# Reciprocals of the softmax sums: VectorE's reciprocal out of PSUM, or ScalarE's exp of minus ln with a Newton step

## The chip, the core and the metric

The kernel runs on one core of one Trainium2 chip. Its engines work through queues of their own and wait for each other by semaphores: TensorE (PE in the profile; its weight loads are PEld), VectorE (DVE), ScalarE (ACT), GpSimd (POOL) and SyncE (SP), which here only issues transfers (DMA). The metric is the time of one execution on the device in microseconds.

## The reference

Two blocks follow each other. The first is attention over 4 batches, 8 heads, 768 positions and 64 dimensions per head, in which a query sees only the keys whose hash (6 bits from a random projection) is equal to its own:

```python
q_bits = (np.einsum('bhsd,dk->bhsk', q, proj) > 0).astype(np.int64)
k_bits = (np.einsum('bhsd,dk->bhsk', k, proj) > 0).astype(np.int64)
...
scores = np.where(q_bucket[:, :, :, None] == k_bucket[:, :, None, :], scale * (q @ k.T), -1e9)
attn = np.exp(scores - np.max(scores, axis=-1, keepdims=True))
attn = attn / (np.sum(attn, axis=-1, keepdims=True) + 1e-09)
x = attn @ v
```

The second block is an MLP mixer on the result, put together as 4 x 768 x 512: `u = x + (relu(x.T @ w_tok1) @ w_tok2).T` over the positions, then `u + relu(u @ w_ch1) @ w_ch2` over the channels. The result is float32; the weights come as 64-bit numbers and are converted on the core.

## The kernel before, in words

The heads are worked on two at a time: 16 pairs of heads, numbered n. Fourteen of them go through the main loop of `attention` (L998), one turn each; the other two ("sorted") are computed by another method whose pieces are put between the turns. After the loop come the token block and the channel block of the mixer, which take the rest of the time (the attention ends at about 300 us).

A pair's 768 queries are worked on in two halves of 384 (`Half`). For each half there are six blocks of 128 keys, and a block holds both heads: 128 keys x (2 x 384) queries, with the keys on the partitions. One turn of the loop issues, in this order, to each engine's queue:

- `scores` (L484 to L518): TensorE computes the twelve blocks of scores into PSUM (L501), ScalarE turns each into exponentials in SBUF (`exponential`, L412). A score block takes a slot of the ring of four PSUM slots (`bank_pair`, L269, tag `sc`, `bufs=4`). The second block is cut in two pieces, so there are thirteen such slots a turn.
- `add` and `add_last` (L444 to L457): VectorE adds up the exponentials over the six blocks of each half, so that 128 partial sums per query are left (`esd`).
- `sums` (L528): for the pair before, TensorE multiplies the partial sums with a matrix of ones (L534). The result `ps` (named `hash` in the profile, after its slot of the same ring) is 128 partitions x 384: four groups of 32 equal rows, in the order head 0 half 0, head 0 half 1, head 1 half 0, head 1 half 1. The other bank of this slot takes the hash bits of the next pair (`Hash`, L342), which VectorE reads (`spread`, L364 and L365) and DMAs spread.
- `sums` ends on ScalarE: `near = exp(-ln(ps))` (L538, L539).
- `newton` (L542): VectorE makes a Newton step on `near` (L547, L549), and ScalarE copies rows of 32 partitions (L555) so that every one of the 128 rows has the reciprocals of both halves. `rec` is 128 x 2 x 384. In the turns 6 and 10, which hold pieces of the sorted pairs, `newton` is called earlier (L1029), ahead of `add_last` and of transposes on VectorE.
- `weigh` (L459) for half 0 and later for half 1: TensorE multiplies the exponentials with the values into the accumulator `acc` (L468), which takes the next slot of the same ring. ScalarE takes the numerators out of it (`vsum` L477, `num` L478).
- Between them VectorE converts a piece of a weight matrix from 64-bit numbers to float32 (`weights.join`, L187 to L196, and `weights.end`, L206), and it forms the quotients (`divide`, L559) for the pair before. In every other turn it transposes results for a bounce through memory (`bounce`, L233).

A PSUM slot is used anew once its readers are through. So the slot of the sums comes free when `newton` has read it, and that of the accumulator when the numerators are out. The order of the queues is the order in which this Python code issues the instructions; nothing reorders it.

The signs are arranged around the Newton step: it gives minus the reciprocal, since `(t - 2) * near` with `t = ps * near` is negative, and so the numerators are taken with `scale=-1.0` (L479), and a constant in the column that is summed along with the values is `-EPS` (L979).

Of the kernel before, what the change touches and what calls it, by code (L numbers as in the profile page):

```python
# [36 lines left out]
F32 = mybir.dt.float32  # L37
# [4 lines left out]
ALU = mybir.AluOpType  # L42
ACT = mybir.ActivationFunctionType
# [5 lines left out]
def kernel(  # L49
# [16 lines left out]
    nc = tc.nc  # L66
    P = 128
    B, NP, _, _, S = qk.shape
    D = 64
# [8 lines left out]
    HALF = S // 2  # L78
# [10 lines left out]
    EPS = 2.0**-70  # L89
# [168 lines left out]
    def attention(pool, psum, W1, W2, x0):  # L258
        first_bits = x0.rearrange("p r c -> p (r c)")[:, :S].bitcast(BF16).rearrange("p (w s) -> p w s", w=2)
        bitrows = [pool.tile([P, S + HALF], BF16, name=f"bits{n}", tag=f"bits{n}", bufs=1) for n in range(2)]  # L260
        exps = pool.tile([P, 2 * NR, 2, HALF + 1], F32, name="exps", tag="exps", bufs=1)
# [7 lines left out]
        def bank_pair(name):  # L269
            return psum.tile([P, 2, 512], F32, name=name, tag="sc", bufs=4)  # L270

        def load_qk(n):
            if n >= NREG:
                return
            b, hp = pairs[n]
            t = pool.tile([P, 2 * (S + HALF)], F32, name="qk", tag="qk", bufs=3)
            if n:
                nc.sync.dma_start(out=t, in_=qk_rows[b, hp])
            else:
                t = t[:, : 2 * S].rearrange("p (w s) -> p w s", w=2)  # L280
                for i in (1, 0):
                    nc.sync.dma_start(out=t[:, i, :HALF], in_=qk[b, hp, :, i, :HALF])
                nc.sync.dma_start(out=t[:, :, HALF:], in_=qk[b, hp, :, :, HALF:])
            loaded[n] = [t, None, None]
# [14 lines left out]
        def apart(made, group):  # L299

            tc.declare_no_dep(made.ins, group=group, reason="another bank of the same tile")
# [100 lines left out]
        class Half:  # L402
# [56 lines left out]
            def weigh(self, to):  # L459

                _, vn, vsum = loaded[self.n]
                columns = HALF if self.half else HALF + 1
                acc = to[:, self.half, :columns]
                for c in range(NR):
                    e = exps[:, NR * self.half + c, :, :columns]
                    for i in range(2):
                        for d in range(0, D, 32):
                            made = nc.tensor.matmul(  # L468
                                acc[D * i + d : D * i + d + 32], vn[:, i, c, d : d + 32], e[:, i],
                                start=(c == 0), stop=(c == NR - 1),  # L470
                            )
                            if self.half:
                                apart(made, f"num{self.n}")
                if self.half == 0:
                    nums[self.n] = pool.tile([P, 2, HALF], F32, name="num", tag="num", bufs=2)
                    vsum = loaded[self.n][2] = pool.tile([P, 1], F32, name="vsum", tag="vsum", bufs=2)
                    tc.add_to_no_dep_group(f"num{self.n}", nc.scalar.copy(vsum, acc[:, HALF:]).ins)  # L477
                made = nc.scalar.activation(  # L478
                    nums[self.n][:, self.half], acc[:, :HALF], ACT.Identity, scale=-1.0, bias=vsum,  # L479
                )  # L480
                if self.half == 0:
                    tc.add_to_no_dep_group(f"num{self.n}", made.ins)
# [37 lines left out]
        nums = {}  # L520

        class Quotients:
# [5 lines left out]
            def sums(self, ps):  # L528

                ps = ps[:, :HALF]  # L530
                for i in range(2):
                    for h in range(2):
                        at = 32 * (2 * i + h)
                        nc.tensor.matmul(  # L534
                            ps[at : at + 32], ones, self.halves[h].d[:, i], start=True, stop=True,
                        )
                near = pool.tile([P, HALF], F32, name="near", tag="near", bufs=1)
                tc.add_to_no_dep_group(f"sums{self.n}", nc.scalar.activation(near, ps, ACT.Ln).ins)  # L538
                nc.scalar.activation(near, near, ACT.Exp, scale=-1.0)  # L539
                self.ps, self.near = ps, near  # L540

            def newton(self):  # L542

                ps, near = self.ps, self.near
                rec = self.rec = pool.tile([P, 2, HALF], F32, name="rec", tag="rec", bufs=1)
                t = rec[:, 1]
                nc.vector.tensor_tensor(t, ps, near, op=ALU.mult)  # L547
                for h in range(2):
                    nc.vector.scalar_tensor_tensor(  # L549
                        rec[:, h], t, 2.0, near, op0=ALU.subtract, op1=ALU.mult,  # L550
                    )
                for i in range(2):
                    for h in range(2):
                        at, other = D * i + 32 * h, D * i + 32 * (1 - h)
                        nc.scalar.copy(rec[other : other + 32, h], rec[at : at + 32, h])  # L555

            def divide(self):
                b, hp = pairs[self.n]
# [33 lines left out]
        sorting, made = pool.tile([P, sum(widths.values())], F32, name="sorting", tag="sorting", bufs=1), {}  # L592
# [383 lines left out]

        nc.scalar.preload_act_table_set("natural_log_exp_and_others")
        nc.vector.memset(first_bits[:, 0], 0.0)
        nc.gpsimd.memset(exps[:, :, :, HALF:], -EPS)  # L979
        load_qk(1)  # L980
        constants = prepare_bits()

# [1 line left out]
        for _ in range(6):  # L984
# [6 lines left out]
            bufs=2,  # L991
# [6 lines left out]
        for n in range(NREG):  # L998
# [26 lines left out]
            acc = bank_pair("acc")  # L1025
# [1186 lines left out]
    def attention_and_tokens(W1, W2, x0):  # L2212
        inside(attention, W1, W2, x0)
        pool = late.enter_context(tc.tile_pool(name="late", bufs=1, side="right", reuse_waits="tile"))
        SW1 = big["SW1"] = pool.tile([P, 3, NCB // 2, DCH // 2], F32, name="SW1")
        TA = big["TA"] = pool.tile([P, 2, NCB // 2, TT], F32, name="TA")
        n = NHT * DM

        def second_tile(i):
            return pool.tile([P, (n, n * 3 // 4)[i]], F32, name=f"second{i}", tag=f"second{i}", bufs=1)  # L2220

        WC2 = second["WC2"] = second_tile(0).rearrange("p (k c) -> p k c", k=NHT)
        second["SW2"] = second_tile(1).rearrange("p (i k c) -> p i k c", i=3, k=NHT // 2)
        second["tile"] = second_tile

        def weights(pool):
            return Conversion(pool, [(w_ch2, WC2, 3, (0, NHT))], bufs=3)

        def jobs(conversion):
            early, late = weight_sums(  # L2230
                WC1, SW1, slice(0, NCB // 2), slice(NCB // 2, NCB), slice(0, DCH // 2), slice(DCH // 2, DCH),
            )
            return [
                lambda: (early(), late()),
                *[conversion.one] * (NHT * DM // NW),
            ]

        SW2 = second["SW2"].rearrange("p i k c -> p i (k c)")
        places = [SW2[:, i] for i in range(3)]
        inside(tokens, W1, W2, x0, weights, jobs, [TA[:, 0], None, TA[:, 1], None], places)  # L2240
# [100 lines left out]
```

## Time and profile before

| What | Value |
|---|---|
| median of 2 runs | 774.15 us (772.04 to 776.27) |
| the profiled execution | 774.78 us |
| its span on the core | 773.0 us |
| granted TensorE clock | 1.0 |
| busy: PE, PEld | 758.4 us, 507.7 us |
| busy: DVE, ACT, POOL | 673.6 us, 443.4 us, 187.7 us |
| exponentials L412 on ScalarE | 126.0 us in 181 instructions |
| copies L555 on ScalarE | 28.5 us in 56 instructions |

The span is the time from the first to the last instruction that the profile shows; the time of the execution is 1.8 us longer. A group's row in the profile names the line, the engine, the operation, the tile written and the tiles read, the shapes and the count; then the busy time in us and the mean of one in ns, and after the bar the time for which the engine stood idle just before these instructions, with what ended it. A row of the order in time has the start in us from the start of the span, the length in us, and the same names; rows that follow each other and are alike are merged, with their count, so that the length covers them all and the small gaps between. A TensorE row's end is modelled, and neighbouring matmuls overlap.

### The profile page before, as it was taken

To read this page: it belongs to the slowest core of one execution; us is meant where nothing else is said; L and a number is where in the kernel's file an instruction comes from. 1 tells how busy PE (TensorE), PEld (TensorE's weight loads), DVE (VectorE), ACT (ScalarE), POOL (GpSimd) and SP (SyncE) were. 2 spreads that over 40 slices of the span, in tenths; PEclk is the share of its full clock that TensorE was granted. 3 is DMA by queue.
4 is the path that set the end of the run, shared out by engine and by line. 5 is a ranking of instruction groups with operands and counts; after the bars stand their busy time and mean duration, and the time that the engine had idled before them with its cause. 6 is when DMAs were issued, how large, how long until landed. Compare 5 with 4: busy or idle time off the path is not lost.

```text
span 773.0 us, 14558 instructions
## 1 busy us (share of the span) xinstructions
PE 758.4 (98%) x5549; PEld 507.7 (66%) x5549; DVE 673.6 (87%) x965; ACT 443.4 (57%) x826; POOL 187.7 (24%) x248
## 2 busy tenths in 40 slices
PE   8999999999999999999999999999999999999997
PEld 4555556565556554455444468888877888886886
DVE  5798999899998998999687798998899799889884
ACT  5576777777777773333222326566766666675331
POOL 2306760547752530011211101210000221000001
PEclk9999999999999999999999999999999999999999
DMA  7455488654765479795696996899576695850565
GB/s 254 173 194 152 153 254 264 177 186 143 164 249 118 143 187 249 265 228 96 113 333 213 345 391 233 254 246 267 171 222 208 235 242 147 241 157 7 203 155 132
DMA packets 129802, 157.80 MB, mean 204 GB/s; under 512 B 56000, under 2 KB 99520, under 8 KB 127808
## 3 DMA queue, kind: packets, MB, share of 16 engines
q1 hardware_dynamic: 115664, 127.32, 51.9%
q0 software_dynamic: 12528, 28.86, 15.9%
q8 instruction: 45, 0.74, 0.4%
q10 hardware_dynamic: 1536, 0.65, 0.3%
q14 instruction: 29, 0.24, 0.1%
HBM read 107.71 MB, written 40.67 MB: 192 GB/s over the span
## 4 chain that ended last, share of the span: by engine, by line
PE 49%; issue 20%; DVE 16%; DMA 6%; SPq 4%; POOL 2%; ACT 2%; DVEq 0%; POOLq 0%; ACTq 0%
PE b L1323 27%; PE sc L501 9%; PE acc L468 7%; DVE esd L457 2%; DMA seen<-in_qk 1%; PE sc L423 1%; DVE size L196 1%; POOL seen L2140 1%; DVE unit L195 1%; SPq L238 1%; PE sacc L873 1%; DMA qk<-in_qk_rows 1%; SPq L919 1%; SPq L806 1%; DMA XT<-second 1%
## 5 line engine op out<-in xcount | busy, mean ns | idle before, releaser
L1323 PE MATMUL b<-R,second 128*128 128x256 f32 (+1 forms) x522 | 132.0, 409 | 0.8 <-ACT c L1329 0.8
L412 ACT ACTIVATE exps<-sc 128x768 f32<-128x768 f32 (+1 forms) x181 | 126.0, 765 | 5.9 <-PE sc L501 3.8
L501 PE MATMUL sc<-qk 32*128 32x384 f32 (+1 forms) x1352 | 119.5, 457 | 0.0
L1323 PEld LDWEIGHTS b<-R,second 128*128 128x128 f32 x522 | 99.0, 190 | 29.7 <-issue 16.5
L468 PE MATMUL acc<-exps,vn 128*32 128x385 f32 (+1 forms) x1344 | 111.7, 486 | 0.0
L501 PEld LDWEIGHTS sc<-qk 32*128 32x128 f32 x1352 | 92.7, 185 | 15.0 <-issue 3.2
L1329 ACT COPY c<-b 128x256 f32<-128x256 f32 (+1 forms) x96 | 40.2, 426 | 79.3 <-PE b L1323 66.1
L468 PEld LDWEIGHTS acc<-exps,vn 128*32 128x32 f32 x1344 | 43.7, 109 | 61.7 <-issue 60.0
L457 DVE TENSOR_TENSOR esd<-esd,exps 128x768 f32<-128x768 f32 x70 | 67.0, 958 | 6.8 <-DVE esd L457 1.0
L789 POOL DMA_INDIRECT table<-XT,sorting x48 | 60.8, 1266 | 23.7 <-issue 11.0
L377 POOL DMA_DIRECT2D bits<-XT x78 | 38.8, 504 | 108.7 <-DVE XT L365 56.5
L1323 PE MATMUL b<-XT,WC 128*128 128x256 f32 (+1 forms) x208 | 61.0, 428 | 0.0
L501 PE MATMUL sc<-bits 32*128 32x384 bf16 (+1 forms) x338 | 49.1, 311 | 0.7 <-ACT num L478 0.6
L1323 PEld LDWEIGHTS b<-XT,WC 128*128 128x128 f32 x208 | 39.5, 190 | 15.4 <-issue 10.3
L1323 PE MATMUL b<-XT,SW 128*128 128x256 f32 (+1 forms) x164 | 47.0, 410 | 0.0
L453 DVE TENSOR_TENSOR esd<-esd,exps 128x768 f32<-128x768 f32 x42 | 40.3, 960 | 4.4
L1196 PE MATMUL t<-x,W 128*128 128x512 f32 x96 | 42.1, 594 | 0.3 <-DMA x<-bounced 0.3
L2140 POOL DMA_DIRECT2D seen<-in_qk x21 | 13.0, 618 | 108.0 <-ACT seen L2130 71.8
L555 ACT COPY rec<-rec 32x384 f32<-32x384 f32 x56 | 28.5, 510 | 16.4 <-DVE rec L549 13.3
L1323 PEld LDWEIGHTS b<-XT,SW 128*128 128x128 f32 x164 | 31.1, 190 | 9.4 <-issue 4.1
L2033 POOL DMA_DIRECT2D out<-second x7 | 8.7, 1243 | 113.2 <-ACT TB L1329 73.9
L177 ACT ACTIVATE size<-raw 128x768 f32<-128x768 f32 x20 | 18.7, 935 | 26.8 <-DMA bits<-XT 16.2
(330 smaller groups left out, 1458.3 us busy)
## 6 DMA issues: line engine op xcount, KB each, us to landing
second<-left SPq DMA_DIRECT2D x20, 768.0 KB
qk<-in_qk_rows SPq DMA_DIRECT2D x13, 1152.0 KB
raw<-in_moe_w_ch SPq DMA_DIRECT2D x16, 768.0 KB
second<-left SPq DMA_DIRECT2D x18, 576.0 KB
seen<-in_qk POOLq DMA_DIRECT2D x21, 384.0 KB, 5.3
WC<-hidden_left SPq DMA_DIRECT2D x18, 448.0 KB
x<-bounced SPq DMA_DIRECT2D x4, 1536.0 KB
XT<-second POOLq DMA_DIRECT2D x8, 768.0 KB, 6.5
```

The costliest lines, as they stand in the source:

```text
L377: queue.dma_start(out=to[at : at + 2 * BITS, half[j]], in_=g[of : of + 2 * BITS])
L412: return nc.scalar.activation(e[:, :, columns], sc, ACT.Exp, scale=SCALE)
L453: nc.vector.tensor_tensor(self.d, self.d, e, op=ALU.add)
L457: nc.vector.tensor_tensor(self.d, self.d, e, op=ALU.add)
L468: made = nc.tensor.matmul(acc[D * i + d : D * i + d + 32], vn[:, i, c, d : d + 32], e[:, i], start=(c == 0), stop=(c == NR - 1),)
L501: nc.tensor.matmul(made[j, piece][:, i], k[at : at + 32, ks], q[at : at + 32], start=part < 0, stop=part == 1,)
L555: nc.scalar.copy(rec[other : other + 32, h], rec[at : at + 32, h])
L789: nc.gpsimd.indirect_dma_start(out=tables[2 * w + i], out_offset=bass.IndirectOffsetOnAxis(ap=self.at[:, x : x + 1], axis=0), in_=row, in_ ...
L1196: nc.tensor.matmul(ps, W1[:, r, P * j : P * j + P], x[:, r], start=(r == 0), stop=(r == NR - 1),)
L1323: nc.tensor.matmul(ps, left(k), right(k), start=start and k == ks[0], stop=stop and k == ks[-1], skip_group_check=True,)
L1329: nc.scalar.copy(c, ps)
L2140: nc.gpsimd.dma_start(out=t, in_=qk[pairs[n][0], pairs[n][1], :, i])
```

## The change

The logarithm, the exponential and the Newton step give way to VectorE's reciprocal operation, which reads the sums in PSUM once, for 128 partitions x 384 elements, and writes into one half of `rec`. The row copies on ScalarE are ordered anew, since now one instruction has written the reciprocals of all four groups of rows into the same columns: six copies a turn in place of four. The sign of the numerators and of the constant column is turned, as the reciprocal is positive. The two sorted pairs keep their own logarithm, exponential and Newton step (L868 to L889).

```diff
@@ -476,7 +476,7 @@
                 made = nc.scalar.activation(
-                    nums[self.n][:, self.half], acc[:, :HALF], ACT.Identity, scale=-1.0, bias=vsum,
+                    nums[self.n][:, self.half], acc[:, :HALF], ACT.Identity, bias=vsum,
                 )
@@ -534,25 +534,18 @@
-                near = pool.tile([P, HALF], F32, name="near", tag="near", bufs=1)
-                tc.add_to_no_dep_group(f"sums{self.n}", nc.scalar.activation(near, ps, ACT.Ln).ins)
-                nc.scalar.activation(near, near, ACT.Exp, scale=-1.0)
-                self.ps, self.near = ps, near
+                self.ps = ps

             def newton(self):

-                ps, near = self.ps, self.near
                 rec = self.rec = pool.tile([P, 2, HALF], F32, name="rec", tag="rec", bufs=1)
-                t = rec[:, 1]
-                nc.vector.tensor_tensor(t, ps, near, op=ALU.mult)
-                for h in range(2):
-                    nc.vector.scalar_tensor_tensor(
-                        rec[:, h], t, 2.0, near, op0=ALU.subtract, op1=ALU.mult,
-                    )
+                made = nc.vector.reciprocal(rec[:, 0], self.ps)
+                tc.add_to_no_dep_group(f"sums{self.n}", made.ins)
                 for i in range(2):
-                    for h in range(2):
-                        at, other = D * i + 32 * h, D * i + 32 * (1 - h)
-                        nc.scalar.copy(rec[other : other + 32, h], rec[at : at + 32, h])
+                    low, high = (slice(at, at + 32) for at in (D * i, D * i + 32))
+                    for rows in (low, high):
+                        nc.scalar.copy(rec[rows, 1], rec[high, 0])
+                    nc.scalar.copy(rec[high, 0], rec[low, 0])
...
@@ -976,7 +969,7 @@
-        nc.gpsimd.memset(exps[:, :, :, HALF:], -EPS)
+        nc.gpsimd.memset(exps[:, :, :, HALF:], EPS)
```

## The prediction

> **What bounds the kernel now.** I read the page first: its span and its busy shares.
>
> ```profile
> span 773.0 us, 14558 instructions
> PE 758.4 (98%) x5549; PEld 507.7 (66%) x5549; DVE 673.6 (87%) x965; ACT 443.4 (57%) x826; POOL 187.7 (24%) x248
> ```
>
> TensorE is busy 98% of the span. The change touches only the attention pairs, which fill the first 300 us, so the second view is the busy time of each engine in two stretches there.
>
> ```profile
> 160.00:178.00 18.00, 18.00 (x246) 10.59 (x238) 17.04 (x22) 13.62 (x24) 11.56 (x13) 1.00 0.44 155
> 178.00:197.00 19.00, 19.00 (x256) 11.61 (x258) 17.22 (x23) 14.51 (x25) 13.69 (x15) 1.00 0.54 162
> ```
>
> The columns after the length are PE, PEld, DVE, ACT, POOL, then the granted clock. TensorE has no gap, at clock 1.00; VectorE has under 2 us to spare in a pair, and ScalarE 4.4 us. So TensorE sets the pace, with VectorE close behind. Busy time doesn't tell who waits for whom, so the third view is one pair in order of time. VectorE first (start, length):
>
> ```profile
> 179.64 0.35 DVE L364 TENSOR_SCALAR XT<-hash 64x192 bf16<-64x192 f32 x1 [0.45 <-PE hash L348]
> ...
> 184.09 0.56 DVE L547 TENSOR_TENSOR rec<-hash,near 128x384 f32<-128x384 f32 x1
> 184.69 1.17 DVE L549 SCALAR_TENSOR_TENSOR rec<-rec,near 128x384 f32<-128x384 f32 x2
> 185.77 0.55 DVE L187 TENSOR_SCALAR unit<-size 128x768 uint32<-128x768 uint32 x1
> ...
> 188.71 0.95 DVE L559 TENSOR_TENSOR XT<-num,rec 128x768 f32<-128x768 f32 x1
> ...
> 192.21 0.91 DVE L448 SCALAR_TENSOR_TENSOR esd<-exps 128x768 f32<-128x768 f32 x1
> ...
> 199.25 0.34 DVE L364 TENSOR_SCALAR XT<-hash 64x192 bf16<-64x192 f32 x1
> ...
> 203.33 0.56 DVE L547 TENSOR_TENSOR rec<-hash,near 128x384 f32<-128x384 f32 x1
> ```
>
> Then ScalarE in the same pair, where the copies of the reciprocals (L555) stand ahead of the numerators (L478), and those ahead of the next pair's exponentials (L412):
>
> ```profile
> 179.23 0.50 ACT L538 ACTIVATE near<-hash 128x384 f32<-128x384 f32 x1
> 179.76 0.53 ACT L539 ACTIVATE near<-near 128x384 f32<-128x384 f32 x1
> ...
> 185.29 2.15 ACT L555 COPY rec<-rec 32x384 f32<-32x384 f32 x4 [1.05 <-DVE rec L549]
> 187.47 0.16 ACT L477 COPY vsum<-acc 128x1 f32<-128x1 f32 x1
> 187.66 1.05 ACT L478 ACTIVATE num<-acc,vsum 128x384 f32<-128x384 f32 x2
> 188.60 1.57 ACT L412 ACTIVATE exps<-sc 128x384 f32<-128x384 f32 x3
> 190.42 7.32 ACT L412 ACTIVATE exps<-sc 128x768 f32<-128x768 f32 x10 [0.25 <-PE sc L501]
> ```
>
> And TensorE at the start of the next pair's scores and at their end:
>
> ```profile
> 188.76 0.34 PE L501 MATMUL sc<-bits 32*128 32x384 bf16 x2
> ...
> 196.51 0.85 PE L534 MATMUL hash<-esd,ones 128*32 128x384 f32 x8
> ```
>
> Score blocks take four PSUM slots in turn, and sums and numerators take slots of the same ring. The third block of a pair (188.76) gets the slot that held the numerators' accumulator, and the last numerator ended at 187.66 + 1.05 = 188.71. It starts 0.05 us later: here the end of L478 already releases TensorE. So there is a second loop, nearly as long as TensorE's: reciprocals on VectorE, copies and numerators on ScalarE, the slot, scores on TensorE, exponentials, the sums of the exponentials, and the reciprocals again. What lengthens it shows in the time.
>
> **The change part by part.** The price of one instruction, from the rows grouped by tile:
>
> ```profile
> L549 DVE SCALAR_TENSOR_TENSOR rec<-rec,near x28: 557/558/573, 41.7 to 295.7; 128x384 f32<-128x384 f32 x28
> L538 ACT ACTIVATE near<-hash x14: 482/498/504, 35.8 to 291.4; 128x384 f32<-128x384 f32 x14
> L539 ACT ACTIVATE near<-near x14: 522/526/527, 36.3 to 292.0; 128x384 f32<-128x384 f32 x14
> L547 DVE TENSOR_TENSOR rec<-hash,near x14: 550/558/559, 41.1 to 294.5; 128x384 f32<-128x384 f32 x14
> L555 ACT COPY rec<-rec x56: 507/510/513, 42.3 to 297.3; 32x384 f32<-32x384 f32 x56
> ```
>
> The loop over pairs computes them in its turns 1 to 13, each for the pair before, and a fourteenth time behind the last sums.
>
> Removed on ScalarE: logarithm and exponential, 0.50 + 0.53 = 1.03 us a pair. They run at 179.23, and ScalarE then waits for VectorE until 185.29 apart from DMA issues and a conversion, so they hide in that idle time: removing them is worth nothing. If that idle time were gone they would be worth 1.03.
>
> Added on ScalarE: two copies more (six for four). At 2.15/4 = 0.54 us each, gap included, 1.07 us a pair, and these do lie in the loop, ahead of L477 and L478. All six now read rows that one instruction writes, so the first waits for its end; before, the first copy began 185.29 - 184.09 = 1.20 us after the start of L547.
>
> Removed on VectorE: three instructions, 184.09 to about 185.86, 1.77 us. Added: one reciprocal of 128x384 out of PSUM. The trace of before holds no such operation. The lower bound is one pass, as L547, 0.56 us. For more than one pass a second length is needed:
>
> ```profile
> L457 DVE TENSOR_TENSOR esd<-esd,exps 128x768 f32<-128x768 f32 x70 | 67.0, 958 | 6.8 <-DVE esd L457 1.0
> ```
>
> From 384 to 768 elements the time goes from 0.558 to 0.958, so a pass over 384 costs 0.40 on a fixed 0.16. Every VectorE row here adds, multiplies, compares, shifts or moves, each done in one pass; the digits of a quotient depend on those found before, and the kernel wants the accuracy for which it now spends a Newton step (L547 to L551) behind the table functions. A fraction has 24 bits: at one bit a pass it would be 24 passes, 0.16 + 24 x 0.40 = 9.76 us, the upper bound. By plain nearness the row of L547 would be taken; I take a value between, eight passes of three bits: 0.16 + 8 x 0.40 = 3.36 us. That is a choice on the nature of the operation, not a reading, and it carries the forecast; the one-pass price is the first rival.
>
> [...]
>
> Now the loop, from the start of L547 at 184.09. Reciprocal until 187.45. Six copies of 0.54: until 190.66, 3.2 later than before (187.44). L477 and L478 took from 187.44 to 188.71, 1.27: now until 191.93. The third block of scores starts there, not at 188.76: TensorE stands 3.2 us, and the sums (196.51 - 188.76 = 7.75 later) come at about 199.7. Spread (L364) follows the sums' start by 1.6 (as 179.64 follows 178.05 below), so at 201.3. VectorE's own queue: conversion until 190.4, L559 when the copies end, 190.7, L448 188.71 to 192.21 later by the same 3.5, 194.2, and L364 7.04 behind it, 201.2. Both say 201.3. From L364 to the next L547 it was 203.33 - 199.25 = 4.08; the next reciprocal starts at 205.4, not 203.33: **2.1 us** a pair that ends in transposes or like work on VectorE.
>
> A pair without those:
>
> ```profile
> 165.52 0.56 DVE L547 TENSOR_TENSOR rec<-hash,near 128x384 f32<-128x384 f32 x1
> ...
> 169.06 1.05 ACT L478 ACTIVATE num<-acc,vsum 128x384 f32<-128x384 f32 x2
> ...
> 178.05 0.85 PE L534 MATMUL hash<-esd,ones 128*32 128x384 f32 x8
> ```
>
> Here the numerators end at 170.11, now at 165.52 + 3.36 + 3.21 + 1.27 = 173.36. Scores then run 7.75 to 181.1, L364 is at 182.7, and L547 follows 4.1 to 4.45 later, at about 186.9 and not at 184.09: **2.8 us**.
>
> Two turns hold sorted work (6 and 10): their reciprocal is put early on VectorE, ahead of transposes, and ScalarE's two extra copies stay on the way: 1.1 us each, with bounds 0 (TensorE's weighing of about 7.8 us covers) and 2.7 (1.6 on VectorE and 1.07 on ScalarE in a row). The last two reciprocals have no next scores behind them:
>
> ```profile
> PE hash L534 <- DVE rec L547: 1.5, 1, 1.5
> ```
>
> Once the last sums already wait for VectorE, so its lateness shows; the weight sums and transposes behind it are partly awaited by transfers. Together 2 us, between 0 and twice 3.2. The sign changes (a scale left out, a positive constant set once) change no instruction's size: nothing. No DMA is moved, added or removed; SP's fetches behind the spread's bits start as much later as L364 does and are in the loop's shift.
>
> Sum: 4 turns without transposes (1, 3, 7, 11) x 2.8 = 11.2; 6 with them (2, 4, 5, 8, 9, 12) x 2.1 = 12.6; 2 x 1.1 = 2.2; last two 2.0. That is 28.0 us. The profiled execution took 774.78 us (span 773.0 and 1.8 around it), 0.6 above the median 774.15. 774.8 + 28.0 = 802.8, **803 us**.
>
> **The rivals.**
>
> One pass (not slower). The reciprocal costs 0.56 as L547 does. VectorE gains 1.77 - 0.56 - 0.03 = 1.2 us a pair; the six copies end at 184.09 + 0.59 + 3.21 = 187.89, 0.45 later than before, and so do the numerators. Pairs held by VectorE (six) gain some 0.6 each, until TensorE holds them again; pairs held by the loop (four) lose 0.4 each, the last two 0.5 each: -3.6 + 1.6 + 1.0 = -1.0 us, **774**, between 771 and 778. For it speak all VectorE rows, none of which costs more than one pass; against it, that none of them divides. It decides below the price at which the loss reaches 2% (15.5 us): the sum rises 28 us for 2.8 us of price, ten to one, so at 0.56 + 1.55 = 2.1 us, five passes.
>
> [...]
>
> Twelve passes, two bits each: 0.16 + 12 x 0.40 = 4.96 us, 1.6 more than forecast, ten pairs and the four others at about a third: 1.6 x 13 = 21 us more, **824**. VectorE, with under 2 us to spare in a pair, would be the bound throughout. Nothing in the profile speaks for or against beyond the nature of division.
>
> A real gain. VectorE's saving would have to pass wholly to the end: 14 x 1.2 = 16.8 us, 758. Against it, TensorE has no gap in the two stretches above, and so can't give back more than the few waits it has.
>
> **How the numbers follow.** A measurement of this kernel can tell about 2% from no change. Several passes as forecast (six to ten, 793 to 813): 0.61. One pass or few, 771 to 789: 0.31. Twelve or more: 0.06. A real gain: 0.02. The likeliest case's own range, with the bounds on the sorted and last pairs, is 790 to 818. Of cases on both sides of 2% the range must take in the one pass: 771 to 820, which leaves out the gain, most of the twelve passes and a little at either edge. Slower by over 2% is the forecast and the twelve passes, 0.67; within 2%, 0.31; faster, 0.02.
>
> **What would show each step.** The reciprocal's row: 3.4 us for 128x384 is right, 0.56 is the first rival, 5.0 the second. Copies: six a pair at 0.51, the first at the reciprocal's end. TensorE: a gap of some 3 us ahead of the third score block (L501 waiting for the numerators) in each ordinary pair. VectorE: L547's successor spaced 21 us, against 18.6 and 19.2 now. The prediction is wrong if the reciprocal takes under 2.1 us, or if it takes 3.4 and TensorE still shows no gap; from the page's slices after the attention nothing should change but its place in time.

## The result, and the profile after

The changed kernel took 794.62 us, median of two runs (793.44 to 795.79), against 774.15 us before: 1.027 times as long, interval 1.0244 to 1.0293. That is 20.5 us slower. The profile is that of the execution of 795.79 us. The ratios here and below were formed apart from the medians and differ a little from their quotients; they leave out one execution, the 822.33 us of e6_after, whose granted clock was 0.980 where its three others had 0.982 to 0.994 and took 809.67 to 814.84 us.

The page first: its span and its busy shares.

```profile
span 794.1 us, 14529 instructions
PE 764.2 (96%) x5549; PEld 511.7 (64%) x5549; DVE 687.4 (87%) x937; ACT 444.0 (56%) x826; POOL 181.6 (23%) x248
```

The span grew by 21.1 us, and TensorE's busy time by only 5.8: most of the new time is TensorE standing. VectorE has 28 instructions fewer (14 x 3 removed, 14 x 1 added) and yet 13.8 us more of work. The rows grouped by tile give most of it (least, median and greatest duration in ns, then the first and the last start):

```profile
L547 ACT COPY rec<-rec x56: 507/510/517, 43.8 to 317.2; 32x384 f32<-32x384 f32 x56
L548 ACT COPY rec<-rec x28: 507/509/513, 44.9 to 317.8; 32x384 f32<-32x384 f32 x28
L542 DVE RECIPROCAL rec<-hash x14: 2549/2556/2559, 41.2 to 312.5; 128x384 f32<-128x384 f32 x14
```

One reciprocal takes 2.556 us, where the three instructions that it replaces took 1.77: 14 x 0.79 = 11 us. It is neither the one pass of 0.56 nor the eight of 3.36 that the forecast took.

TensorE's waits over the attention (total us, times, longest):

```profile
PE sc L501 <- ACT num L478: 17.1, 10, 2.0
PE hash L534 <- DVE rec L542: 2.5, 1, 2.5
```

and the first of these rows before:

```profile
PE sc L501 <- ACT num L478: 0.6, 1, 0.6
```

Score blocks that wait for the numerators: ten times and 17.1 us, where before there was a single wait of 0.6 us. That is the gap that the prediction placed there, at 2 us a turn and not 3. The wait of the last sums grew from 1.5 to 2.5 us.

Two turns by engine (PE, PEld, DVE, ACT, POOL, the granted clock, the DMA share, GB/s):

```profile
170.00:190.00 20.00, 18.02 (x246) 11.07 (x246) 18.00 (x20) 13.41 (x23) 12.04 (x14) 1.00 0.41 143
190.00:211.00 21.00, 19.15 (x256) 11.49 (x248) 19.20 (x22) 14.54 (x25) 12.15 (x14) 1.00 0.49 151
```

TensorE, without a gap before, now stands for 1.98 us of 20 and 1.85 of 21; and VectorE too has 2.0 and 1.8 us to spare. No engine is full: this is what a loop through several engines looks like in busy shares. One turn in order of time shows the loop, VectorE first:

```profile
175.91 2.56 DVE L542 RECIPROCAL rec<-hash 128x384 f32<-128x384 f32 x1
...
181.69 0.96 DVE L552 TENSOR_TENSOR XT<-num,rec 128x768 f32<-128x768 f32 x1 [0.22 <-ACT rec L548]
...
184.42 0.96 DVE L448 SCALAR_TENSOR_TENSOR esd<-exps 128x768 f32<-128x768 f32 x1 [0.90 <-ACT exps L412]
...
192.32 0.35 DVE L364 TENSOR_SCALAR XT<-hash 64x192 bf16<-64x192 f32 x1 [0.73 <-PE hash L348]
...
196.39 2.56 DVE L542 RECIPROCAL rec<-hash 128x384 f32<-128x384 f32 x1
```

ScalarE in the same turn:

```profile
178.50 1.03 ACT L547 COPY rec<-rec 32x384 f32<-32x384 f32 x2 [2.44 <-DVE rec L542]
179.57 0.51 ACT L548 COPY rec<-rec 32x384 f32<-32x384 f32 x1
180.09 1.03 ACT L547 COPY rec<-rec 32x384 f32<-32x384 f32 x2
181.15 0.51 ACT L548 COPY rec<-rec 32x384 f32<-32x384 f32 x1
181.68 0.16 ACT L477 COPY vsum<-acc 128x1 f32<-128x1 f32 x1
181.87 1.05 ACT L478 ACTIVATE num<-acc,vsum 128x384 f32<-128x384 f32 x2
```

And TensorE, from sums to sums:

```profile
170.11 0.85 PE L534 MATMUL hash<-esd,ones 128*32 128x384 f32 x8
...
182.98 0.34 PE L501 MATMUL sc<-bits 32*128 32x384 bf16 x2 [1.98 <-ACT num L478]
...
190.72 0.85 PE L534 MATMUL hash<-esd,ones 128*32 128x384 f32 x8
```

ScalarE stands 2.44 us until the reciprocal is out (175.91 + 2.56 = 178.47), makes six copies in a row until 181.66, and takes out the numerators until 181.87 + 1.05 = 182.92; 0.06 us later TensorE's third score block starts, after a gap of 1.98 us. The stretch from the start of the reciprocal to the end of the numerators is 7.01 us, against 188.71 - 184.09 = 4.62 before (4.59 in most turns). The next reciprocal starts 20.48 us after this one; before, the two spacings in this part were 18.57 and 19.24 (165.52, 184.09, 203.33).

The starts of L534, one in each turn, cut the attention into turns, and their differences show where the time came in. Turn 1 runs from 34.61 to 54.46 before and from 34.72 to 56.50 after.

| us from sums to sums | 1 | 2 | 3 | 4 | 5 | 6 | 7 | 8 | 9 | 10 | 11 | 12 | to the last sums |
|---|---|---|---|---|---|---|---|---|---|---|---|---|---|
| before | 19.85 | 18.66 | 18.35 | 18.34 | 19.95 | 29.94 | 18.35 | 18.46 | 19.22 | 29.38 | 18.35 | 18.34 | 6.24 |
| after | 21.78 | 22.17 | 20.48 | 20.48 | 21.33 | 29.15 | 20.61 | 20.48 | 20.48 | 28.26 | 20.61 | 20.48 | 7.28 |
| longer by | 1.93 | 3.51 | 2.13 | 2.14 | 1.38 | -0.79 | 2.26 | 2.02 | 1.26 | -1.12 | 2.26 | 2.14 | 1.04 |

The sum is 20.2 of the span's 21.1 us; 0.1 lies ahead of the first sums and 0.8 behind the last. The 3.51 of turn 2 holds about 1.7 us of a fall of the granted clock (0.54 and 0.61 in the two windows of 2 us from 70 to 74 us); in another execution of the same instructions (e11_prices below) turn 2 took 20.47.

A turn has three pieces: from the start of the sums to that of the reciprocal (before: of L547), the stretch, and from the end of the numerators to the next sums. In three of the turns they are, in us, before / after:

| turn | sums to reciprocal | stretch | numerators to sums | turn |
|---|---|---|---|---|
| 3 | 5.69 / 5.66 | 4.59 / 7.02 | 8.07 / 7.80 | 18.35 / 20.48 |
| 8 | 6.04 / 5.67 | 4.62 / 7.01 | 7.80 / 7.80 | 18.46 / 20.48 |
| 9 | 6.82 / 5.67 | 4.60 / 7.01 | 7.80 / 7.80 | 19.22 / 20.48 |

The third piece is 7.80 us where the third score block follows the numerators at once (8.28 in turns 1 and 5), and longer where the numerators are out before TensorE comes to that block. In turn 2 of the changed kernel the fall of the clock comes on top. So a turn loses the 7.01 - 4.59 = 2.42 us of the stretch, less the time that TensorE had in hand (0.27 us in turn 3), and less what the reciprocal now starts sooner behind the sums (1.15 us in turn 9).

### The profile page after: what moved, and what is told of

Its sections match the earlier page's. It is cut to its first block, busy times and chain, and to the rows that moved or that the text cites. A ratio compares the mean times of both kernels' runs of the same rounds, so it can differ in the third digit from the quotient of the medians.

```text
span 794.1 us, 14529 instructions
## 1 busy us (share of the span) xinstructions
PE 764.2 (96%) x5549; PEld 511.7 (64%) x5549; DVE 687.4 (87%) x937; ACT 444.0 (56%) x826; POOL 181.6 (23%) x248
## 4 chain that ended last, share of the span: by engine, by line
PE 39%; issue 19%; DVE 12%; ACT 5%; DMA 4%; POOL 2%; SPq 1%; DVEq 0%; POOLq 0%; ACTq 0%
PE b L1316 26%; PE t L1229 4%; PE sc L501 3%; DVE esd L457 3%; PE t L1189 3%; DVE rec L542 2%; ACT rec L547 2%; DMA seen<-in_qk 1%; DVE esd L453 1%; POOL seen L2133 1%; DMA XT<-in_kv_rows 1%; PE acc L468 1%; ACT rec L548 1%; PE sacc L866 1%; DMA XT<-second 1%
## 5 line engine op out<-in xcount | busy, mean ns | idle before, releaser
L501 PE MATMUL sc<-qk 32*128 32x384 f32 (+1 forms) x1352 | 122.9, 463 | 0.0
L468 PE MATMUL acc<-exps,vn 128*32 128x385 f32 (+1 forms) x1344 | 113.4, 491 | 0.0
L501 PEld LDWEIGHTS sc<-qk 32*128 32x128 f32 x1352 | 95.0, 187 | 11.9 <-issue 0.8
L457 DVE TENSOR_TENSOR esd<-esd,exps 128x768 f32<-128x768 f32 x70 | 67.0, 957 | 6.8 <-DVE esd L457 0.6
L501 PE MATMUL sc<-bits 32*128 32x384 bf16 (+1 forms) x338 | 51.8, 313 | 17.2 <-ACT num L478 17.1
L782 POOL DMA_INDIRECT table<-XT,sorting x48 | 55.5, 1155 | 24.9 <-issue 10.7
L547 ACT COPY rec<-rec 32x384 f32<-32x384 f32 x56 | 28.5, 509 | 30.2 <-DVE rec L542 29.7
L501 PEld LDWEIGHTS <-bits 32*128 32x128 bf16 x338 | 21.2, 92 | 30.6 <-issue 25.4
L542 DVE RECIPROCAL rec<-hash 128x384 f32<-128x384 f32 x14 | 35.8, 2556 | 0.3
```

Source lines behind the costliest of these rows:

```text
L457: nc.vector.tensor_tensor(self.d, self.d, e, op=ALU.add)
L468: made = nc.tensor.matmul(acc[D * i + d : D * i + d + 32], vn[:, i, c, d : d + 32], e[:, i], start=(c == 0), stop=(c == NR - 1),)
L501: nc.tensor.matmul(made[j, piece][:, i], k[at : at + 32, ks], q[at : at + 32], start=part < 0, stop=part == 1,)
L542: made = nc.vector.reciprocal(rec[:, 0], self.ps)
L547: nc.scalar.copy(rec[rows, 1], rec[high, 0])
L782: nc.gpsimd.indirect_dma_start(out=tables[2 * w + i], out_offset=bass.IndirectOffsetOnAxis(ap=self.at[:, x : x + 1], axis=0), in_=row, in_ ...
```

## The experiments

Three theories. First, the loop of the prediction: what counts is the length of the stretch from the start of the reciprocal to the end of the numerators, wherever in it the time is added. Second, VectorE's own work: it had under 2 us to spare in a turn, and now has 0.8 us more to do. Third, the two additional copies on ScalarE alone.

The experiments ran on three chips. On the first (e1 to e4) and the second (e5 to e8) the unchanged kernel before took 796.04 and 795.94 us, on the third (e9 to e12) 774.28; so each ratio is to the kernel before on the same chip. Which chip gave the first result is not on record; on the third, e11_prices, the changed kernel with work added behind the attention, repeats the turns of the changed kernel to 0.01 us, turn 2 apart. Turn 1 is the measure for all: in both profiles of the kernel before (the first and that on the second chip) it takes 19.85 us, and in both of the changed kernel 21.78 and 21.77, so that what sets the chips apart doesn't show in it.

**What a reciprocal costs** (e11_prices). Behind the attention, eight reciprocals more, of different width, source and number of partitions:

```diff
         before.divide()
         finish()
+        for n in (96, 192, 384):
+            nc.vector.reciprocal(exps[:, 0, 0, :n], before.ps[:, :n])
+            nc.vector.reciprocal(exps[:, 1, 0, :n], exps[:, 2, 0, :n])
+        nc.vector.reciprocal(exps[:, 3, :, :HALF], exps[:, 4, :, :HALF])
+        nc.vector.reciprocal(exps[:32, 5, 0, :HALF], exps[:32, 6, 0, :HALF])
```

> The changed kernel with eight reciprocals more behind the end of the attention, to price the operation: 96, 192 and 384 elements out of PSUM and out of SBUF, 768 out of SBUF, and 384 on 32 partitions only. From the 2.556 us of 128x384 and a fixed part of 0.16: 2.40 / 384 = 6.25 ns an element, six passes of 1.04. So 0.76, 1.36 and 2.56 us, 4.96 for 768, the same out of SBUF but for a few hundredths, and 2.56 on 32 partitions. If the operation has a start-up of its own, the small ones are longer than that.

The groups by form of VectorE (the tile `hash` is in PSUM, `exps` in SBUF; behind the bar busy us and mean ns of one):

```profile
L542 DVE RECIPROCAL rec<-hash 128x384 f32<-128x384 f32 x14 | 35.8, 2556 | 0.3
...
L1062 DVE RECIPROCAL exps<-exps 128x768 f32<-128x768 f32 x1 | 4.9, 4895 | 0.0
...
L1061 DVE RECIPROCAL exps<-exps 128x384 f32<-128x384 f32 x1 | 2.5, 2495 | 0.0
...
L1060 DVE RECIPROCAL exps<-hash 128x384 f32<-128x384 f32 x1 | 2.5, 2494 | 0.0
...
L1063 DVE RECIPROCAL exps<-exps 32x384 f32<-32x384 f32 x1 | 2.5, 2482 | 0.0
...
L1060 DVE RECIPROCAL exps<-hash 128x192 f32<-128x192 f32 x1 | 1.3, 1295 | 0.0
...
L1060 DVE RECIPROCAL exps<-hash 128x96 f32<-128x96 f32 x1 | 0.7, 719 | 0.0
```

From 384 to 768 elements the time grows by 2400 ns, 6.25 ns an element. Between L547 and L457 of the kernel before (0.558 us for 384 elements, 0.958 for 768) it grows by 400/384 = 1.04 ns an element, the prediction's pass, so the reciprocal takes the time of six such passes on a fixed 0.1 us. The 384 elements took 2494 ns out of PSUM and 2495 out of SBUF, and 2482 on 32 partitions in place of 128. Of the 2.556 us in the loop, then, all but 0.06 show behind the attention as well (2.494 us), and so are the price of the operation itself and not a wait in the loop.

**Without the two additional copies** (e9_four_copies).

```diff
                     for rows in (low, high):
                         nc.scalar.copy(rec[rows, 1], rec[high, 0])
-                    nc.scalar.copy(rec[high, 0], rec[low, 0])
```

> The changed kernel with four copies in place of six: the copy of the low rows' reciprocals to the high rows is left out, so half the quotients take another half's reciprocal. Theory 1, the loop: from the start of the reciprocal to the end of the numerators 7.01 - 1.07 = 5.94 us (before 4.59), and of the 18 us that the changed kernel lies above the kernel before on these chips about 1.07 / 2.42 = 44% go, 8 us: 1.013. Theory 2, VectorE's own work: nothing goes, 1.02. Theory 3, the copies are the whole cost: all goes, 1.00.

785.75 us, 1.0146 (1.013 to 1.0162): 11.5 us above before, and about 9 below the 794.62 of the changed kernel, which was not timed on this chip. ScalarE in turn 3:

```profile
84.43 2.08 ACT L547 COPY rec<-rec 32x384 f32<-32x384 f32 x4 [2.08 <-DVE rec L542]
86.53 0.16 ACT L477 COPY vsum<-acc 128x1 f32<-128x1 f32 x1
86.73 1.05 ACT L478 ACTIVATE num<-acc,vsum 128x384 f32<-128x384 f32 x2
```

VectorE and TensorE's sums of that turn, and TensorE's wait:

```profile
81.84 2.56 DVE L542 RECIPROCAL rec<-hash 128x384 f32<-128x384 f32 x1
```

```profile
76.17 0.85 PE L534 MATMUL hash<-esd,ones 128*32 128x384 f32 x8
...
95.58 0.85 PE L534 MATMUL hash<-esd,ones 128*32 128x384 f32 x8
```

```profile
PE sc L501 <- ACT num L478: 8.4, 10, 1.7
```

The stretch is 86.73 + 1.05 - 81.84 = 5.94 us, 1.07 shorter than with six copies, and the turn takes 19.41 in place of 20.48: 1.07 shorter as well. One for one, as the loop wants it, and turns 1, 4, 7, 8, 11 and 12 are 1.06 or 1.07 shorter too. The copies hold some 44% of the loss (9 of 20.5), so the third theory alone is not enough. The 1.35 us by which the stretch is still longer than before are the reciprocal's: the first copy starts 84.43 - 81.84 = 2.59 us after it, where before it started 1.20 us after L547.

**VectorE's work without the stretch** (e10_before_vector). The kernel before, with 0.55 + 0.26 = 0.81 us of work added to VectorE behind the quotients, where no numerators wait for it; the tile `near` is no longer read there:

```diff
             if before:
                 before.divide()
+                near = before.near
+                nc.vector.tensor_tensor(near, near, near, op=ALU.mult)
+                nc.vector.tensor_tensor(near[:, :96], near[:, :96], near[:, :96], op=ALU.mult)
```

> The kernel before with 0.82 us more work on VectorE in each turn, about what the change adds there (2.56 for 1.77), as two multiplications of a tile that nobody reads any more, put behind the quotients and so outside the stretch from the Newton step to the numerators. Theory 2, VectorE's own work: as the changed kernel, 1.02. Theory 1: the stretch stays 4.59 us; only turns in which VectorE's queue is full pass it on, at most 6 x 0.8 = 5 us: 1.00 to 1.007.

779.78 us, 1.0074 (1.0057 to 1.009): 5.5 us. VectorE in turn 3, and TensorE's sums at its ends:

```profile
79.57 0.56 DVE L547 TENSOR_TENSOR rec<-hash,near 128x384 f32<-128x384 f32 x1
...
85.11 0.55 DVE L1055 TENSOR_TENSOR near<-near 128x384 f32<-128x384 f32 x1
85.70 0.26 DVE L1056 TENSOR_TENSOR near<-near 128x96 f32<-128x96 f32 x1
```

```profile
73.89 0.85 PE L534 MATMUL hash<-esd,ones 128*32 128x384 f32 x8
92.23 0.85 PE L534 MATMUL hash<-esd,ones 128*32 128x384 f32 x8
```

As much work as the changed kernel gives VectorE (it gives it 2.556 - 1.77 = 0.79 more), and the turn takes 18.34 us, as before. What was lost came in turns 2 (19.43), 5 (21.07), 6 (30.32), 9 (20.08) and 10 (29.93) and at the last sums (7.13). So VectorE's work by itself is worth 5.5 us in the kernel before, where the second theory has 1.02 and the first at most 1.007, and it shows in other turns than those in which the changed kernel loses most. It costs through the same loop: in turn 2 the reciprocal starts 7.04 us behind the sums in place of 6.27, the stretch stays, and 7.04 + 4.59 + 7.80 = 19.43.

**The stretch without the reciprocal** (e3_before_six). The kernel before with six copies in place of four (two are done twice):

```diff
                         nc.scalar.copy(rec[other : other + 32, h], rec[at : at + 32, h])
+                    nc.scalar.copy(rec[D * i : D * i + 32, 1], rec[D * i + 32 : D * i + 64, 1])
```

> The kernel before with two copies more in each turn (six for four; the added ones copy the same rows once more), and else unchanged. Theory 1: 1.07 us more in the loop; in turns with transposes VectorE's queue covers it, in the four plain turns about 0.85 us shows, in the two turns with sorted work 1.1: 781 us, between 776 and 785. Theory 2: no VectorE work is added, 774. Theory 3, the copies are what costs: 790 or more.

803.77 us, 1.0115 (1.0077 to 1.0152), 7.7 us, where theory 1 has 7. TensorE's sums at both ends of turn 1:

```profile
35.06 0.85 PE L534 MATMUL hash<-esd,ones 128*32 128x384 f32 x8
55.52 0.85 PE L534 MATMUL hash<-esd,ones 128*32 128x384 f32 x8
```

20.46 us: turn 1 grew by 0.61 us, with the stretch 1.08 longer. Copies alone, with no reciprocal, cost time.

**The price of one pass** (e4_one_pass, and again e8_one_pass). The changed kernel with a copy in place of the reciprocal, so that the division is left out:

```diff
-                made = nc.vector.reciprocal(rec[:, 0], self.ps)
+                made = nc.vector.tensor_copy(rec[:, 0], self.ps)
```

> The changed kernel with a plain VectorE copy of the sums in place of the reciprocal, so that the division is left out; six copies on ScalarE as in the changed kernel. It stands for a reciprocal of one pass, 0.56 us. Theory 1: 774 us, between 771 and 778, as the first rival of the prediction has it. Theory 2: VectorE has 1.2 us less work in a turn than in the kernel before, 765 or less. Theory 3: 790 or more.

> The changed kernel with a plain VectorE copy in place of the reciprocal, division left out, again. Theory 1 on a chip without the unnamed waits: within 0.5% of the kernel before. If it stays 1.8% slower with turns of 18.4 us in its undisturbed part, the rest comes from the unnamed waits; if the turns themselves are 20 us, the six copies cost more than the loop's arithmetic says.

809.63 us, 1.018 (1.0147 to 1.0213), and 802.87 us, 1.0084 (1.0048 to 1.012). Turn 1 of the second shows no loss:

```profile
36.22 0.85 PE L534 MATMUL hash<-esd,ones 128*32 128x384 f32 x8
56.06 0.85 PE L534 MATMUL hash<-esd,ones 128*32 128x384 f32 x8
```

19.84 us, as before (stretch 5.01). The whole times, though, are above what theory 1 has for them, and they differ from each other by more than their intervals. Both were taken on the chips where before takes 796 us, and the losses lie in later turns, which differ there by as much as is looked for (turn 2: 20.96 and 20.05). The numerators aren't what TensorE waits for in them: the third score blocks wait for them 0.2 us in all in the first run and 0.6 in the second. What it is instead, and whether the six copies have a part in it, the runs don't show. What one pass would cost on the third chip was not tried, and this part stays open.

**The chips** (e5_before, e6_after). The two kernels unchanged, on the second chip.

> The kernel before, unchanged, for a profile from the same chip as the runs beside it. On the chip of the first four experiments it took 796 us and not 774, and their profiles show TensorE waiting inside the scores with no releaser ('issue') and short falls of the granted clock, which the first profiles of before and after do not show. If those belong to the chip, this run shows them there and not on a chip where the time is 774.

> The changed kernel, unchanged, beside the kernel before: the measured ratio again, 1.027, so about 20 us more; the waits of the third score block for the numerators some 17 us in total, the loop's turns 20.5 us. If the ratio is 1.01 or less on another chip, the loss depends on the chip and not on the loop alone.

Before 793.07 in this one execution; after 812.80 (median of the three executions that the ratio counts), 1.0186 (1.0135 to 1.0238). The loss is of like size, about 17 us, on a chip where the kernel before takes longer itself. The waits with no releaser show on this chip too (0.8 us in the scores of e5_before), and in no profile of a kernel on the third chip. The one profile of e6_after is of the execution of 822.33 us; in it the third score blocks wait 7.8 us for the numerators and not 17.

**The reciprocal earlier in the queue** (e1_early, e7_early on the changed kernel; e2_before_early, e12_before_early on the kernel before). `newton` is called right behind the sums in every turn, as the sorted turns already do, so that reciprocals and copies start ahead of `add_last`:

```diff
-            if piece:
+            if before:
                 before.newton()
+            if piece:
                 now_at(n, "newton")
...
-            if before and not piece:
-                before.newton()
```

> The changed kernel, with the reciprocal (and its copies behind it) put ahead of the second half's last three additions on VectorE in every turn, where the changed kernel does that in turns 6 and 10 only. The work of every engine stays the same. Theory 1, the loop (reciprocal, copies, numerators, PSUM slot, third score block): the reciprocal starts some 3 us earlier against the numerators, the copies end before TensorE is through with its weighing, and the waits of the third score block (17.1 us in the changed kernel) nearly go: 778 us, between 772 and 784. Theory 2, VectorE's own work (0.8 us more in each turn, wherever it stands): nothing comes back, 793 to 796. Theory 3, the two more copies: as theory 1, since they move along.

> The kernel before with the same move: the Newton step ahead of the second half's last three additions in every turn. Theory 1: the numerators already released TensorE only a few tenths of a us late in some turns, so there is little to win, 770 to 774. Theory 2: nothing changes, 774. If it is slower than 776, the later additions have a cost of their own, and the first run's number has to be read with that.

> The changed kernel with the reciprocal ahead of the second half's last three additions in every turn, again. In the first run it was 1.9% above the kernel before and not at 0.5%, as theory 1 had it, but with TensorE waiting for nothing that the profile names. Theory 1, the loop, on a chip without these waits: 0.5% above the kernel before, between -0.3 and 1.3. Theory 2, VectorE's own work: as the changed kernel, 2.7%.

> The kernel before with the Newton step ahead of the second half's last three additions in every turn, again, in more rounds: it was 1.1% faster than the kernel before on the first chip. Theory 1 has the numerators a few tenths of a us too late in some turns of the kernel before, so 0.990 to 0.998; if it is not faster here, the first run's gain was that chip's.

| kernel | chip | us | ratio to before (interval) |
|---|---|---|---|
| e1_early | first | 810.06 | 1.0189 (1.0154 to 1.0223) |
| e7_early | second | 810.25 | 1.0155 (1.0107 to 1.0203) |
| e2_before_early | first | 788.04 | 0.9888 (0.9847 to 0.9929) |
| e12_before_early | third | 777.05 | 1.0034 (1.0021 to 1.0047) |

TensorE's sums at both ends of turn 1 in e1_early:

```profile
34.89 0.85 PE L534 MATMUL hash<-esd,ones 128*32 128x384 f32 x8
54.74 0.85 PE L534 MATMUL hash<-esd,ones 128*32 128x384 f32 x8
```

TensorE's waits for the numerators over the attention in e1_early:

```profile
PE sc L501 <- ACT num L478: 1.8, 2, 1.3
```

19.85 us: with the reciprocal of 2.56 us and six copies in it, turn 1 takes no longer than before once the stretch starts earlier. And the waits of the third score block go, from 17.1 us to 1.8 (1.6 in e7_early), as the loop has it: only when the numerators come out counts. But the whole time did not come back (810.25 us, beside 812.80 for the changed kernel on the second chip): theory 1's 778 us and 0.5% both missed. The later turns lose it, with waits that the profile puts down to no releaser (4.4 and 3.4 us in the scores), and what the rest is the runs don't show; the order was not tried with the reciprocal on the third chip. For the kernel before, the earlier order gained 8 us on the first chip and lost 2.8 on the third, where a gain was expected, so it is no version to keep: none that ran beats the kernel before on both.

**Turn 1 over five kernels.** The lengthening of the stretch against the lengthening of the turn, both in us, each against the kernel before (stretch 4.59, turn 19.85):

| kernel | stretch | turn |
|---|---|---|
| after | +2.42 | +1.93 |
| e9_four_copies | +1.35 | +0.87 |
| e3_before_six | +1.08 | +0.61 |
| e8_one_pass | +0.42 | -0.01 |
| e10_before_vector | 0 | -0.01 |

In the first three rows the turn grows by the stretch less 0.47 to 0.49 us; in the fourth the stretch grew by less than that, and nothing is lost. One line through kernels that lengthen the stretch on VectorE, on ScalarE or on both. That is the loop with a cover of some 0.48 us, the time that TensorE has in hand in turn 1; in turns 3, 4, 7, 11 and 12 of the kernel before it has 0.14 to 0.27, and in 2, 5, 8 and 9 nothing. The three pieces add up in other turns too: 5.67 + 5.94 + 7.80 = 19.41 in turn 3 of e9_four_copies.

## Why the prediction was right

**The loop** was shown: the turn follows the stretch, by copies alone, by the reciprocal and the copies, and VectorE's work outside of it counts only where it makes the reciprocal start later. The form of the stretch was right to 0.06 us: with the measured price the prediction's terms give 2.56 + 0.03 + 3.21 + 1.27 = 7.07, measured 7.01.

**The price of the reciprocal** was a choice, eight passes and 3.36 us, and it was 0.80 too high. No run shows eight passes: the runs showed 2.556 us, the time of six (6.25 ns an element beside 1.04), and that the digits of a quotient ask for several passes was the author's estimate. The bounds of 0.56 and 9.76 held it, the point of decision (2.1 us) lay below it, and so the sign was right. By the prediction's own rule of ten us of time for one of price, 0.80 less gives 803 - 8 = 795; 794.6 was measured. That the price fell on this side of the point of decision was in part luck: no row of the kernel before spoke for several passes, and the range of 771 to 820 took in both sides. Price apart, then, the sum was right, but partly because its terms made up for each other:

- Turns without transposes (1, 3, 7, 11), 2.8 us each: by the measured price 2.8 - 0.8 = 2.0. Measured 1.93 to 2.26. Right, with the price; the time that TensorE had in hand makes the difference to 2.42.
- Turns with transposes (2, 4, 5, 8, 9, 12), 2.1 us each: by the measured price 1.3. Turns 5 and 9 lost 1.38 and 1.26, but 4, 8 and 12 lost 2.02 to 2.14, as much as the plain ones, and turn 2, without the fall of the clock, 20.47 - 18.66 = 1.81. The step that failed is the split: the 2.1 was counted from VectorE's start at 203.33 (a spacing of 19.24 us from 184.09), where VectorE's queue ran late, and was taken for all six turns, though TensorE's sums, in rows that stood in the prediction, were 196.51 - 178.05 = 18.46 apart, hardly more than in the plain turn. What the lateness covers is how much sooner behind the sums the reciprocal now starts: 1.15 us in turn 9 (6.82 before, 5.67 now) and 1.04 in turn 5, as forecast, but 0.61 in turn 2, 0.37 in turn 8 and 0.01 in turns 4 and 12. VectorE's spacings run from 16.08 to 19.74 us outside the sorted turns of the kernel before; which engine's spacing is the turn has to be read from the one that hardly waits, and that was TensorE.
- Sorted turns (6, 10), +1.1 us each: measured -0.79 and -1.12, the wrong sign. In turn 6 the stretch did grow, by 0.73 us (8.21 to 8.94), but the reciprocal starts 3.29 us behind the sums and not 4.81, most likely because VectorE's queue had time to spare in the longer turns before it (with that queue fuller, in e10_before_vector, it starts 5.59 us behind them). So the numerators come out 0.79 us sooner behind the sums, and that is what the turn gained. In turn 10 the kernel before waits for a transfer and the changed kernel doesn't: the hash products start 1.77 us behind the sums before and 0.67 after, which is 1.10 of the 1.12. The prediction had neither term.
- The end, 2 us: measured 1.04 until the last sums and 0.8 behind them. The wait of the last sums for the reciprocal grew by 1.0, as its row shows.

The rows of the sorted turns on TensorE, where turn 6 waits for the numerators (before, then after) and turn 10 for the transfer (before):

```profile
142.83 2.13 PE L847 MATMUL ss<-x 32*128 32x256 bf16 x38 [1.21 <-ACT num L478]
153.24 2.13 PE L840 MATMUL ss<-x 32*128 32x256 bf16 x38 [0.87 <-ACT num L478]
217.50 0.35 PE L348 MATMUL hash<-qk,projs 128*32 128x192 f32 x1 [0.91 <-DMA qk<-in_qk_rows]
```

**No cover** was wrong by a little. The prediction read from one row, of turn 8, that the numerators' end already releases TensorE, and let the whole lengthening pass in the plain turns too; 0.48 us of it is covered in turn 1, and in turn 7 the 2.42 us made the turn 2.26 longer.

**The copies** came as forecast: six at 0.51, the first 0.03 us behind the reciprocal, 1.07 us more in the stretch, of which e9_four_copies gives the whole back.

**Logarithm and exponential worth nothing** fits the ordinary turns, where ScalarE stands 2.44 us until the reciprocal is there, and the waits of the kernel before have none of VectorE for `near`; it was not tested by itself.

**The rivals.** One pass (774): refuted by the reciprocal's row; that its price would have left no loss is shown in turn 1 alone, where TensorE had the most time in hand. Twelve passes: refuted by the same row. A real gain: VectorE did not save 1.2 us a pair, it got 0.79 us more to do.

## What to carry to other kernels

An exchange of instructions is judged by the length of the chain that it lies in, not by their number and not by the engine's busy share: here three instructions became one, the engine stayed 87% busy, and the time grew by 2.7%. An operation that no row of the trace holds is to be priced by itself before it takes the place of cheap passes; on 384 elements the reciprocal cost 2.56 us, more than four and a half times a multiplication. And where one instruction writes for all partitions what three wrote in the right places, the moves between partitions come on top: two copies of 0.51 us each were worth 9 us over the kernel.

## What the runs showed of the hardware

A reciprocal took 6.25 ns an element between 384 and 768 elements, the time of six passes of 1.04; 384 elements took 2494 ns out of PSUM, 2495 out of SBUF and 2482 on 32 partitions in place of 128 (e11_prices).

The kernel before took 774.28 us on the third chip, and 796.04 and 795.94 on the first and the second. At one place the traces differ in how many matmuls TensorE has in a window of 1 us, at a DMA share of 0.98 to 1.05. Three such windows of the kernel before on the second chip, and then three of the kernel before in the first measurement:

```profile
103.00:104.00 1.00, 1.00 (x22) 0.86 (x19) 0.96 (x2) 0.45 (x1) 1.00 (x1) 1.00 1.01 415
104.00:105.00 1.00, 1.00 (x12) 0.55 (x7) 1.00 (x3) 0.00 (x0) 0.69 (x2) 1.00 0.98 395
105.00:106.00 1.00, 0.90 (x7) 0.36 (x5) 1.00 (x3) 0.58 (x1) 0.91 (x1) 1.00 0.98 395
```

```profile
102.00:103.00 1.00, 1.00 (x22) 0.93 (x18) 1.00 (x3) 0.88 (x2) 0.83 (x1) 1.00 0.99 371
103.00:104.00 1.00, 1.00 (x20) 0.78 (x16) 1.00 (x2) 0.74 (x3) 0.73 (x1) 1.00 0.99 401
104.00:105.00 1.00, 1.00 (x18) 0.80 (x12) 1.00 (x2) 1.00 (x2) 0.00 (x0) 1.00 1.05 416
```

In both, 371 to 416 GB/s are moved at a granted clock of 1.00. In the first measurement TensorE keeps 18 to 22 matmuls in a window; on the second chip it falls from 22 to 12 and 7, though it counts as busy for 0.90 us or more of each. What makes it slow there was not tried; how much of the 22 us between the chips it holds, and why the two traces differ, stay open.
